# Float64 weights to float32: two activations and three integer steps in place of a masked reassembly

## The chip, the cores and the metric

The kernel runs on one core of a Trainium2 chip. The metric is the time of one execution on the device in microseconds; the runs shown are given by their median.

## The reference

Causal attention over 4 batches, 12 heads, 448 positions and head width 64 feeds a gated product: with x the attention's output as 1792 rows of 768,

```python
scores = scale * np.matmul(q, k.transpose(0, 1, 3, 2))      # causal mask, softmax, times v
a = x @ w_a          # 768 x 1536
b = x @ w_b          # 768 x 1536
return (a * b @ w_out).astype(np.float32)                   # 1536 x 768
```

q, k and v come as float32. The three weight matrices come as float64, since the setup multiplies float32 numbers by a float64 scalar.

## The kernel before

**Layout.** The weights are cut into 36 units of 128 partitions by 768 columns: 24 for w_a and w_b (a pair for each of 12 blocks of the inner width) and 12 for w_out. A unit arrives as 64-bit words, which the kernel reads as pairs of 32-bit words: `t.t[:, :, 0]` are the low words, `t.t[:, :, 1]` the high ones, each 8 bytes from the next.

**Conversion.** `convert_unit` (line 358) makes one float32 unit out of one float64 unit. Line 371 masks the exponent out of the high words, line 373 the fraction, and sets the hidden one; line 376 rebiases the exponent on ACT; line 378 adds the low words to the fraction as a floating-point number; line 380 puts the sign in front of the exponent; line 383 multiplies fraction and exponent. The result goes into `w_32`, and by DMA into `w_keep` in memory, from which later uses load it again. The buffers are rings: three for the 64-bit words (`w_64`), two for `w_e`, two for `w_m`, three for `w_32`. In the rows of the trace below, buffer numbers and what follows them are left out, so `w_64` and `w_32` both read `w`.

**Splitting and products.** `split` (line 396) makes each float32 weight into a high part (`w_hi`, copied on ACT, line 315) and the remainder (`w_lo`, subtracted on DVE, line 331). `products` (line 742, the matmul is line 746) then does three passes for each block of 128: high times high, high times low, low times high. The activations are split in the same manner.

**Stages.** Up to about 90 us the attention of batches 0 and 1 runs (`scores`, `turn`, `values`): scores on PE, maxima on DVE (line 492), exponentials on ACT (line 498), scaling on ACT or POOL (lines 520 and 521), transposes on PE (line 554) with their copies on ACT or DVE (lines 315 and 323), and products with v (lines 576 and 598). From about 67 us the products of these batches with the weights begin, use by use (`uses`, line 1007), and the attention of batches 2 and 3 is woven in between them, one pair of heads for every twelve steps (`attend`, line 1070), until about 244 us. Behind that there are products alone. In each use of the first half one unit is converted for a use soon to come (`convert_next`) and, by the table `EXTRA`, in twelve of them one more, whose result is only stored for later.

**Order.** Nothing is issued in program order. Each operation is noted with its engine, a planned duration, what it reads and writes, and (for DVE operations that share a port with POOL) the mode "x". `Plan.order` (line 142) is a list scheduler: it runs through the planned durations and picks for each engine, in general, the earliest operation in program order among those that are ready. The order that it finds is then issued as it is, so on the chip each engine executes a fixed sequence. Loads and stores go through SP's queue, sums into memory through POOL's.

Of the kernel before, what the change touches and what calls it, by code (L numbers as in the profile page):

```python
# [9 lines left out]
F32 = mybir.dt.float32  # L10
F32R = mybir.dt.float32r
U32 = mybir.dt.uint32
AF = mybir.ActivationFunctionType
ALU = mybir.AluOpType
# [4 lines left out]
P = 128  # L19
# [6 lines left out]
UW = KT * P  # L26
# [229 lines left out]
def causal_attention_then_gated_product(  # L256
# [9 lines left out]
    nc = tc.nc  # L266
    plan = Plan()
# [4 lines left out]
    def sb(tag, n, shape, dt=F32):  # L272
        return plan.ring(tag, n, lambda i: sbuf.tile(shape, dt, tag=f"{tag}{i}", name=f"{tag}{i}"))
# [32 lines left out]
    w_m = sbuf.tile([P, 2, UW], U32, tag="w_m", name="w_m")  # L306
# [27 lines left out]
    def load(nbytes, o, i, reads, writes, by=None):  # L334
        plan.op("sp", dma_ns(nbytes), lambda: (by or nc.sync).dma_start(out=o(), in_=i()), reads, writes)
# [6 lines left out]
    w_64, w_32, w_parts = [], [], []  # L342
# [14 lines left out]

    def convert_unit(besides=False):
        u, t = w_64.pop(0)
        e, m, wt = sb("w_e", 2, [P, UW], U32), plan.ring("w_m", 2, lambda i: w_m[:, i]), sb("w_32", 3, [P, UW])  # L360

        def low():
            return t.t[:, :, 0]

        def high():
            return t.t[:, :, 1]

        def r():
            return m.t.bitcast(F32)

        plan.op("dve", 470, lambda: nc.vector.tensor_scalar(  # L371
            out=e.t, in0=high(), scalar1=0x7FF00000, scalar2=None, op0=ALU.bitwise_and), [t], [e], "x")
        plan.op("dve", 470, lambda: nc.vector.tensor_scalar(
            out=m.t, in0=high(), scalar1=0x000FFFFF, scalar2=0x00100000,
            op0=ALU.bitwise_and, op1=ALU.bitwise_or), [t], [m], "x")
        plan.op("act", 735, lambda: nc.scalar.activation(  # L376
            e.t, e.t, AF.Copy, bias=-896.0 * 2**23, scale=8.0), [e], [e])
        plan.op("dve", 869, lambda: nc.vector.scalar_tensor_tensor(
            out=r(), in0=m.t, scalar=2.0**32, in1=low(), op0=ALU.mult, op1=ALU.add), [m, t], [m], "x")
        plan.op("dve", 869, lambda: nc.vector.scalar_tensor_tensor(  # L380
            out=e.t, in0=high(), scalar=0x80000000, in1=e.t,
            op0=ALU.bitwise_and, op1=ALU.bitwise_or), [t, e], [e], "x")
        plan.op("dve", 869, lambda: nc.vector.scalar_tensor_tensor(  # L383
            out=wt.t, in0=r(), scalar=2.0**-52, in1=e.t.bitcast(F32),
            op0=ALU.mult, op1=ALU.mult), [m, e], [wt], "x")
        load(P * UW * 4, lambda: w_keep[u], lambda: wt.t, [wt], [("keep", u)])
        if not besides:
            w_32.append(wt)
# [371 lines left out]
    def convert_one(besides=False):  # L760
        convert_unit(besides)
        load_next()
# [430 lines left out]
```

## Time and profile before

| what | value |
|---|---|
| median of the 3 runs shown | 617.97 us |
| lowest and highest | 617.84 and 619.04 us |
| span of the profiled execution | 616.9 us |
| median less that span | 1.1 us |
| PE busy | 610.7 us (99%) |
| DVE busy | 550.2 us (89%) |
| ACT busy | 385.7 us (63%) |
| POOL busy | 81.9 us (13%) |
| conversions: first and last start on DVE | 31.7 and 364.3 us |

The span runs from the first to the last instruction of one profiled execution, whose own time is not listed apart from it; the 1.1 us are how far the median of the runs stands above it. Busy times are sums over the whole span, and the stages differ: a share of the whole says little about any one of them. The ends of matmuls are modelled, so a busy PE is not by itself PE at its peak.

### The profile page before, as it was taken

Reading aid. Unit: us, or ns where it says so; the run is one execution under the profiler, and the core shown is the slowest. Engines: PE = TensorE matmul, PEld = TensorE weight load, DVE = VectorE, ACT = ScalarE, POOL = GpSimd, SP = SyncE. Lnnn points to the kernel's source line nnn. Section 1 sums busy time; section 2 is a strip of 40 time slices with the busy share of each in tenths; the row PEclk is TensorE's granted clock in tenths of the full one; section 3 lists DMA queues with packets and bytes.
Section 4 is the critical chain, followed back from the end, with each engine's and each line's share of the span. In section 5 each row is a group of like instructions: output and inputs, shape, how many; then the busy total and the mean of one; then the engine's idle time right before and its main releaser. Section 6 shows DMA issues by size and latency. Waiting matters only on the chain.

```text
span 616.9 us, 11539 instructions
## 1 busy us (share of the span) xinstructions
PE 610.7 (99%) x4027; PEld 543.1 (88%) x4027; DVE 550.2 (89%) x1237; ACT 385.7 (63%) x932; POOL 81.9 (13%) x140
## 2 busy tenths in 40 slices
PE   8999999999999999999999999999999999999997
PEld 6666778888888888999999999999999999999997
DVE  7799999999999999899889996788999768889984
ACT  6989969978898887454445545344455434455530
POOL 3775112210011111000000122000000000000030
PEclk9999999999999999999999999999999999999999
DMA  8879889687776778972122678321113432122354
GB/s 312 255 180 290 233 246 316 187 284 241 250 261 210 257 262 311 340 260 78 53 76 100 173 167 172 81 68 62 52 52 120 154 112 76 52 74 78 104 91 100
DMA packets 46858, 104.70 MB, mean 170 GB/s; under 512 B 5456, under 2 KB 31440, under 8 KB 46800
## 3 DMA queue, kind: packets, MB, share of 16 engines
q1 hardware_dynamic: 41904, 96.16, 47.2%
q0 software_dynamic: 4608, 7.34, 8.5%
q8 instruction: 32, 0.52, 0.3%
q10 hardware_dynamic: 288, 0.46, 0.2%
q14 instruction: 26, 0.21, 0.1%
HBM read 70.52 MB, written 33.42 MB: 168 GB/s over the span
## 4 chain that ended last, share of the span: by engine, by line
PE 96%; ACT 2%; DVE 1%; DMA 1%; issue 0%
PE m L746 66%; PE t L746 7%; PE t L554 6%; PE s L746 4%; PE pv L576 3%; PE s L483 3%; PE t L483 2%; PE pv L746 2%; PE m L598 2%; PE pv L598 1%; ACT p L498 1%; PE m L483 1%; ACT early L498 1%; DMA raw<-kT 1%; DVE w_e L371 0%; ACT pt L315 0%
## 5 line engine op out<-in xcount | busy, mean ns | idle before, releaser
L746 PE MATMUL m<-x_hi,w_hi 128*128 128x448 f32 x360 | 134.8, 374 | 0.0
L746 PE MATMUL m<-x_hi,w_lo 128*128 128x448 f32 x360 | 130.6, 363 | 0.0
L746 PE MATMUL m<-x_lo,w_hi 128*128 128x448 f32 x360 | 130.1, 361 | 0.0
L315 ACT ACTIVATE w_hi<-w 128x384 fp32r<-128x384 f32 (+1 forms) x96 | 57.5, 599 | 31.0 <-PE m L746 13.1
L746 PEld LDWEIGHTS m<-x_hi,w_lo 128*128 128x128 f32 x360 | 67.5, 188 | 5.0
L746 PEld LDWEIGHTS m<-x_hi,w_hi 128*128 128x128 f32 x360 | 67.6, 188 | 4.5 <-issue 0.2
L746 PEld LDWEIGHTS m<-x_lo,w_hi 128*128 128x128 f32 x360 | 67.6, 188 | 4.0
L315 ACT ACTIVATE mid<-m 128x448 f32<-128x448 f32 x72 | 38.9, 540 | 51.0 <-PE m L746 43.4
L498 ACT ACTIVATE p<-p,st 128x448 f32<-128x448 f32 (+6 forms) x126 | 62.5, 498 | 9.7 <-DVE st L492 9.6
L315 ACT ACTIVATE w_hi<-w_e_s 128x384 fp32r<-128x384 f32 x72 | 37.3, 521 | 45.8 <-PE m L746 25.0
L331 DVE TENSOR_TENSOR w_lo<-w,w_hi 128x384 fp32r<-128x384 f32 (+1 forms) x96 | 63.0, 656 | 2.6 <-ACT w_hi L315 2.6
L340 POOL DMA_DIRECT2D out<-mid x20 | 17.6, 898 | 347.5 <-ACT mid L315 335.2
L521 POOL TENSOR_SCALAR p<-p,st 128x256 f32<-128x256 f32 (+6 forms) x56 | 38.6, 726 | 136.8 <-ACT p L498 69.5
L746 PE MATMUL m<-g_hi,w_hi 128*128 128x448 f32 (+2 forms) x150 | 54.6, 364 | 0.0
L746 PE MATMUL m<-g_hi,w_lo 128*128 128x448 f32 (+2 forms) x150 | 53.8, 359 | 0.0
L746 PE MATMUL m<-g_lo,w_hi 128*128 128x448 f32 (+2 forms) x150 | 53.7, 358 | 0.0
L331 DVE TENSOR_TENSOR w_lo<-w_e_s,w_hi 128x384 fp32r<-128x384 f32 x72 | 39.9, 554 | 13.9 <-ACT w_hi L315 13.3
L315 ACT ACTIVATE pt<-t 128x512 f32<-128x512 f32 x72 | 39.8, 575 | 9.2 <-PE t L554 8.7
L746 PE MATMUL m<-p_x,w_hi 128*128 128x448 f32 x144 | 43.7, 363 | 0.0
L315 ACT ACTIVATE g_hi<-mid 128x448 fp32r<-128x448 f32 x42 | 24.1, 575 | 21.9 <-DVE mid L331 21.9
L380 DVE SCALAR_TENSOR_TENSOR w_e<-w,w_e 128x768 uint32<-128x768 uint32 x36 | 34.7, 965 | 0.7 <-ACT w_e L376 0.5
L383 DVE SCALAR_TENSOR_TENSOR w<-w_m,w_e 128x768 f32<-128x768 f32 x36 | 35.3, 979 | 0.0
(182 smaller groups left out, 1478.2 us busy)
## 6 DMA issues: line engine op xcount, KB each, us to landing
w<-w SPq DMA_DIRECT2D x36, 768.0 KB, 6.2
w<-w_keep SPq DMA_DIRECT2D x48, 384.0 KB, 3.1
w_keep<-w SPq DMA_DIRECT2D x36, 384.0 KB, 5.2
raw<-qT SPq DMA_DIRECT2D x24, 224.0 KB, 4.1
raw<-kT SPq DMA_DIRECT2D x22, 224.0 KB, 4.5
v<-v SPq DMA_DIRECT2D x24, 192.0 KB, 4.3
out<-mid SPq DMA_DIRECT2D x20, 224.0 KB, 3.9
out<-mid POOLq DMA_DIRECT2D x20, 224.0 KB, 4.2
```

The costliest lines, as they stand in the source:

```text
L315: return nc.scalar.activation(o(), i(), AF.Copy)
L331: plan.op(engine, ns, lambda: e.tensor_tensor(out=o(), in0=a(), in1=b(), op=op), reads, writes, "f" if banks.intersection(reads) else "x")
L340: lambda: nc.gpsimd.dma_start(out=o(), in_=i(), accum_op=ALU.add), reads, writes, "d")
L380: plan.op("dve", 869, lambda: nc.vector.scalar_tensor_tensor(out=e.t, in0=high(), scalar=0x80000000, in1=e.t, op0=ALU.bitwise_and, op1=ALU ...
L383: plan.op("dve", 869, lambda: nc.vector.scalar_tensor_tensor(out=wt.t, in0=r(), scalar=2.0**-52, in1=e.t.bitcast(F32), op0=ALU.mult, op1=A ...
L483: x = nc.tensor.matmul(at[r][0].t[to * D:(to + 1) * D, at[r][1]], q[:, r * D:(r + 1) * D], k[:, 0:D * (r + 1)], start=True, stop=True)
L498: return nc.scalar.activation(view(r), view(r), AF.Exp, bias=st.t[:, nm, r:r + 1], scale=-1.0, accum_out=st.t[:, sm, r:r + 1],)
L521: return nc.gpsimd.tensor_scalar(out=view(r), in0=view(r), scalar1=st.t[:, rc, r:r + 1], scalar2=1.0, op0=ALU.mult, op1=ALU.mult)
L554: x = nc.tensor.matmul(t.t[:, P * i:P * (i + 1)], of, swapped if rs[0] in CROSSED else ident, is_transpose=True, start=True, stop=True,)
L576: r = nc.tensor.matmul(ps.t[j * D:(j + 1) * D, 128 * c:S], vt.t[:, c, j, :], parts[n].t[:, j, o:o + count, :].rearrange("p i d -> p (i d)" ...
L598: r = nc.tensor.matmul((ps, more)[row].t[j * D:(j + 1) * D, at:at + count * D], v, parts[n].t[rows, j, o:o + count, :].rearrange("p i d -> ...
L746: r = nc.tensor.matmul(ps.t[:, at], a[:, i, :], x()[:, at], start=first and n == 0, stop=last and n == 2, skip_group_check=part)
```

## The change

The unit is converted in another way. ACT reads the high words as float32 numbers and scales them by 2 to the power of -112, which moves the exponent's bias, and reads the low words as integers and scales them by 2 to the power of -29, rounded to integers. DVE shifts the scaled high words left by 3 bits, puts the sign bit of the high words in front, and adds the rounded low words as integers. There are two ACT operations where there was one, and three DVE operations where there were five. The buffers and their rings stay, with `w_e` holding the rounded low words; the planned durations are those of like operations before. The store into `w_keep` and all that uses the units stay as they are.

```diff
     def convert_unit(besides=False):
         u, t = w_64.pop(0)
-        e, m, wt = sb("w_e", 2, [P, UW], U32), plan.ring("w_m", 2, lambda i: w_m[:, i]), sb("w_32", 3, [P, UW])
-
-        def low():
-            return t.t[:, :, 0]
+        y, m, wt = sb("w_e", 2, [P, UW], U32), plan.ring("w_m", 2, lambda i: w_m[:, i]), sb("w_32", 3, [P, UW])
 
         def high():
             return t.t[:, :, 1]
 
-        def r():
-            return m.t.bitcast(F32)
-
+        plan.op("act", 735, lambda: nc.scalar.activation(
+            m.t.bitcast(F32), high().bitcast(F32), AF.Copy, scale=2.0**-112), [t], [m])
+        plan.op("act", 735, lambda: nc.scalar.activation(y.t, t.t[:, :, 0], AF.Copy, scale=2.0**-29), [t], [y])
         plan.op("dve", 470, lambda: nc.vector.tensor_scalar(
-            out=e.t, in0=high(), scalar1=0x7FF00000, scalar2=None, op0=ALU.bitwise_and), [t], [e], "x")
-        plan.op("dve", 470, lambda: nc.vector.tensor_scalar(
-            out=m.t, in0=high(), scalar1=0x000FFFFF, scalar2=0x00100000,
+            out=m.t, in0=m.t, scalar1=3, scalar2=None, op0=ALU.logical_shift_left), [], [m], "x")
+        plan.op("dve", 869, lambda: nc.vector.scalar_tensor_tensor(
+            out=m.t, in0=high(), scalar=0x80000000, in1=m.t,
             op0=ALU.bitwise_and, op1=ALU.bitwise_or), [t], [m], "x")
-        plan.op("act", 735, lambda: nc.scalar.activation(
-            e.t, e.t, AF.Copy, bias=-896.0 * 2**23, scale=8.0), [e], [e])
-        plan.op("dve", 869, lambda: nc.vector.scalar_tensor_tensor(
-            out=r(), in0=m.t, scalar=2.0**32, in1=low(), op0=ALU.mult, op1=ALU.add), [m, t], [m], "x")
-        plan.op("dve", 869, lambda: nc.vector.scalar_tensor_tensor(
-            out=e.t, in0=high(), scalar=0x80000000, in1=e.t,
-            op0=ALU.bitwise_and, op1=ALU.bitwise_or), [t, e], [e], "x")
-        plan.op("dve", 869, lambda: nc.vector.scalar_tensor_tensor(
-            out=wt.t, in0=r(), scalar=2.0**-52, in1=e.t.bitcast(F32),
-            op0=ALU.mult, op1=ALU.mult), [m, e], [wt], "x")
+        plan.op("dve", 869, lambda: nc.vector.tensor_tensor(
+            out=wt.t.bitcast(U32), in0=m.t, in1=y.t, op=ALU.add), [m, y], [wt], "x")
         load(P * UW * 4, lambda: w_keep[u], lambda: wt.t, [wt], [("keep", u)])
```

## Rows read from the trace of the kernel before

**Rows 1.** The page: span, and busy us, share and instructions of PE's line.
```profile
span 616.9 us, 11539 instructions
...
PE 610.7 (99%) x4027; PEld 543.1 (88%) x4027; DVE 550.2 (89%) x1237; ACT 385.7 (63%) x932; POOL 81.9 (13%) x140
```

**Rows 2.** The chain that ended last, in order of time: start, us, what.
```profile
244.55 28.01 PE m L746 x139
...
272.59 186.19 PE m L746 x929
```

**Rows 3.** Stages: length; busy us of PE, PEld, DVE, ACT, POOL; clock, DMA, GB/s.
```profile
36.00:67.40 31.40, 31.40 (x333) 21.22 (x330) 30.62 (x108) 28.90 (x92) 17.74 (x32) 1.00 0.87 234
67.40:92.20 24.80, 24.80 (x179) 19.90 (x178) 23.35 (x42) 20.24 (x50) 2.57 (x3) 1.00 0.91 253
92.20:244.50 152.30, 152.30 (x1332) 133.89 (x1329) 146.48 (x353) 133.62 (x346) 23.24 (x25) 1.00 0.77 257
244.50:280.00 35.50, 35.48 (x180) 32.91 (x177) 32.43 (x57) 18.05 (x35) 0.00 (x0) 1.00 0.81 282
```

**Rows 4.** Waits of PE's weight loads, 20 to 245 us: total us, times, longest.
```profile
PEld s L483 <- issue: 7.0, 41, 0.2
...
PEld t L554 <- ACT pt L315: 1.2, 1, 1.2
...
PEld t L554 <- DVE st L492: 0.2, 1, 0.2
...
PEld s L483 <- DMA raw<-kT: 0.2, 1, 0.2
```

**Rows 5.** DVE in order of time, around 31 and 228 us: start, us, instruction.
```profile
31.69 1.97 DVE L371 TENSOR_SCALAR w_e<-w 128x768 uint32<-128x768 uint32 x1
...
227.34 0.95 DVE L383 SCALAR_TENSOR_TENSOR w<-w_m,w_e 128x768 f32<-128x768 f32 x1
228.21 0.56 DVE L371 TENSOR_SCALAR w_e<-w 128x768 uint32<-128x768 uint32 x1
228.68 0.56 DVE L373 TENSOR_SCALAR w_m<-w 128x768 uint32<-128x768 uint32 x1
```

**Rows 6.** ACT in order of time, around 114 us.
```profile
114.16 1.57 ACT L376 ACTIVATE w_e<-w_e 128x768 uint32<-128x768 uint32 x2
```

**Rows 7.** Groups by line and shape: count, busy us, mean ns; idle before.
```profile
L315 ACT ACTIVATE w_hi<-w 128x384 fp32r<-128x384 f32 x72 | 37.3, 518 | 27.5 <-PE m L746 11.7 <-PE t L746 10.6 <-ACT w_hi L315 2.7
...
L383 DVE SCALAR_TENSOR_TENSOR w<-w_m,w_e 128x768 f32<-128x768 f32 x36 | 35.3, 979 | 0.0
L378 DVE SCALAR_TENSOR_TENSOR w_m<-w_m,w 128x768 f32<-128x768 uint32 x36 | 35.1, 974 | 0.1
...
L376 ACT ACTIVATE w_e<-w_e 128x768 uint32<-128x768 uint32 x36 | 30.1, 841 | 4.4 <-DVE w_e L371 4.2
...
L331 DVE TENSOR_TENSOR w_lo<-w,w_hi 128x768 fp32r<-128x768 f32 x24 | 23.2, 965 | 0.0
...
L373 DVE TENSOR_SCALAR w_m<-w 128x768 uint32<-128x768 uint32 x36 | 20.3, 564 | 0.0
L315 ACT ACTIVATE w_hi<-w 128x768 fp32r<-128x768 f32 x24 | 20.2, 840 | 3.5 <-DVE w L383 1.7 <-PE m L746 1.4 <-PE t L483 0.3
```

**Rows 8.** Stages, line 376 on ACT alone: busy us (instructions); clock, DMA, GB/s.
```profile
36.00:67.40 31.40, 1.68 (x2) 1.00 0.87 234
67.40:92.20 24.80, 4.20 (x5) 1.00 0.91 253
92.20:244.50 152.30, 19.14 (x23) 1.00 0.77 257
```

**Rows 9.** Waits of SP's queue, 92.2 to 244.5 us.
```profile
SPq L335 <- DVE w_e L380: 32.3, 12, 6.4
```

**Rows 10.** Waits of ACT, 92.2 to 244.5 us.
```profile
ACT p L498 <- DVE st L492: 6.4, 11, 1.5
ACT pt L315 <- PE t L554: 6.4, 11, 1.6
```

## The prediction

> **What bounds the kernel now.** I read the page first. PE is busy 610.7 of 616.9 us [rows 1], but the ends of matmuls are modelled, so that figure doesn't show that PE is at its limit. The chain of waits in order of time does. From 244.55 us on it is PE alone: 929 matmuls in 186.19 us are 0.2004 us each, behind 139 in 28.01 us at 0.2015 [rows 2]. The reader is to see that nothing but matmuls is left to shorten there: whatever the change does after 244 us costs and gains nothing unless PE is made to wait.
>
> Next the table by stage [rows 3]. From 36 to 244.5 us PE's busy time equals the length of each stretch, and the waits of PE's weight loads [rows 4] say the same from 20 us on: the longest sum, 7.0 us in 41 pieces, is "issue" (it waited for no other engine), the longest wait for ACT is one of 1.2 us, for DVE one of 0.2 us, for a DMA one of 0.2 us. So PE is the bound from about 20 us to the end, and the conversion's first instruction comes at 31.7 us [rows 5]. Before that the change has nothing to touch.
>
> The same table shows what stands close behind PE. In the long stretch from 92.2 to 244.5 us, where the second half of the attention is woven into the products, DVE is busy 146.48 of 152.30 us (96.2%) and ACT 133.62 us (87.7%). In the stretch after it ACT is busy 18.05 of 35.50 us.
>
> **The change, part by part.** Profiled durations overlap the next instruction's start, so I price an instruction by its distance to the next one. On DVE a scalar_tensor_tensor of 768 columns takes 228.21 - 227.34 = 0.87 us and a tensor_scalar 228.68 - 228.21 = 0.47 us [rows 5]. On ACT two conversions in a row take 1.57 us, of which the last shows its full 0.84: 0.73 us each [rows 6].
>
> *DVE, removed*: two tensor_scalar and three scalar_tensor_tensor per unit, 2 x 0.47 + 3 x 0.87 = 3.55 us. *DVE, added*: one shift (tensor_scalar), one scalar_tensor_tensor, one tensor_tensor add. No shift and no integer add is in the trace. The shift is nearest to the masks, also 32-bit tensor_scalar of 768 columns, one of them 564 ns [rows 7]: 0.47 us; if it ran at the pace of the two-input instructions, 0.87. The add is nearest to the tensor_tensor of 768 columns at 965 ns [rows 7]: 0.87 us. New sum 0.47 + 0.87 + 0.87 = 2.21 us (bound above 2.61). DVE loses 1.34 us per unit (0.94 at least). In the long stretch 23 units pass [rows 8]: 23 x 1.34 = 30.8 us, and DVE falls from 146.48 to about 116 us of 152.3.
>
> *ACT, removed*: one activation per unit, 0.73 us. *ACT, added*: two, the scaling of the high words and the rounding of the low ones. Both are Copy with a scale over 768 columns, like the one removed (841 ns) and like the split of a weight at 840 ns [rows 7], but they read every second word, 8 bytes apart, which no ACT row here does from SBUF. On DVE a read of that step costs nothing: the instruction that reads the low words takes 974 ns, the one with three contiguous operands 979 [rows 7]. I take 0.73 us each, so ACT gains 0.73 us per unit. The bound above is ACT at half pace: 384 more columns cost 840 - 518 = 322 ns [rows 7], so 768 column times more are 0.64 us an instruction.
>
> ACT's sum by stretch, with the units of [rows 8] and the busy times of [rows 3]: 36 to 67.4 us, 28.90 + 2 x 0.73 = 30.4 of 31.4 us; 67.4 to 92.2, 20.24 + 5 x 0.73 = 23.9 of 24.8; 92.2 to 244.5, 133.62 + 23 x 0.73 = 150.4 of 152.3, that is 98.8%. So the change moves the place of the nearest engine behind PE from DVE to ACT, and nearer than DVE was. Of ACT and DVE together the long stretch loses 14 us of work.
>
> What hides the added ACT work is PE's own stream. PE needs ACT for the exponentials, the transposes' copies and the weight splits, but products of weights already split lie between them, and a conversion is needed only uses later. Without that cover the cost would be all of what ACT can't hold.
>
> The Trainium skill speaks on both sides here. "ScalarE: Activation LUTs", section "Rules for kernel authors", gives a plain multiply to VectorE rather than ScalarE, and the rows agree in direction: 0.47 us on DVE against 0.73 on ACT. "Perfetto Trace Analysis", section "Optimizing Scalar/DVE Operations", allows the move when DVE is saturated. By the first rule the change puts work on the dearer engine, by the second on the freer one; the sum above goes by the rows, where DVE at 96.2% is still not what PE waits for.
>
> **Waits and queues.** The order of each engine is made anew from the planned costs, so the whole interleaving between 30 and 280 us can shift. Each conversion used to begin on DVE and visit ACT in its middle; now it begins on ACT, which needs only the loaded words, and ends with three DVE steps in a row. An activation that waits (for the load, or for a buffer of w_m or w_e that two units before still hold) has exponentials and PSUM copies queued behind it on ACT, and PE waits for those. On SP the next load of 64-bit words waits for the last reader of the old ones: 32.3 us in 12 waits for line 380 [rows 9], with the attention's loads queued behind. After the change that reader is the sign step on DVE (or the rounding on ACT, if it is later), which two DVE steps fewer precede. I cost this at nothing, covered as now by loads issued early: PE waits 0.2 us for DMAs in all [rows 4]; if the cover were gone, it would be the longest of these waits, 6.4 us, once. The stores of the converted weights don't move.
>
> What could be gained: ACT now idles 6.4 us for the maxima from DVE and 6.4 us for transposes from PE in the long stretch [rows 10]. A relieved DVE takes away the former, and this is what makes room for the new activations.
>
> **The rivals.** *Hidden (my forecast).* PE stays fed. For: ACT's work still fits into every stretch, the freed DVE shortens ACT's own waits, and DVE at 96.2% costs PE next to nothing today. I add one uncovered activation, 0.73 us, in the stretch from 36 us on, where few products are ready yet (between 0 and the two units' 1.46): 616.9 + 0.7 = 617.6 us of span, or with the 1.1 us by which the median 617.97 stands above the profiled span, 618.7.
>
> *ACT becomes the bound (other side: slower).* Place: 92.2 to 244.5 us. If ACT can be kept busy there no better than DVE is now, its 150.4 us take 150.4 / 0.962 = 156.3 us: 4.0 us more, 622.0. The same comes out if only the 6.4 us that it waits for transposes stay: 156.8, or 4.5 more. It decides as soon as ACT idles more than 152.3 - 150.4 = 1.9 us there. For: today it idles 18.7 us in that stretch, and each engine executes a fixed order, in which PE must stop at a late transposition even with products behind it. Against: conversions need nothing but loaded words, so they fill ACT's gaps; late ACT work can move past 244.5 us, where 17 us are idle. Upper bound, if both waits of [rows 10] stay: 163.2, or 10.9 more.
>
> *The strided reads slow ACT.* 2 x 0.644 us per unit make 23 x 1.288 = 29.6 us more, ACT needs 180.0 us in the stretch, 27.7 too many: about 646. Against: the DVE rows above. The Trainium skill has a rule by which this happens: "Vector Engine (DVE) Microarchitecture Reference", section "5.2 Measured stream behaviour on trn2 (trn3 not measured)", wants runs of two adjacent words for the full rate. The rows of the strided DVE reads don't bear it out at this step, and for ACT no row here shows it.
>
> *Faster.* A lighter DVE would have to end waits of PE. All of PE's waits for other engines between 20 and 245 us are a few us at most, those for DVE 0.2 us apiece [rows 4]; a luckier order might give back 1.5 us: 616.5.
>
> **How the numbers follow.** Hidden 0.50, ACT bound 0.38, strided reads 0.04, faster 0.08. About 0.2%, 1.2 us, is what a measurement here can tell from no change (the three runs shown lie between 617.84 and 619.04). Hidden lies within it (617.2 to 619.2 by its own bounds); the ACT bound and the strided reads are slower, 0.42 together; faster 0.08. The predicted time is that of the hidden case, 618.7. The range goes from 617.2, which leaves out most of the faster cases, to 623.0, which takes in the ACT bound at 622.0 and 622.5 and leaves out its far end and the strided case.
>
> **What would show it.** Right: two new activations at about 0.84 us each, the shift at about 0.56, sign and add at about 0.96; DVE near 116 us of the long stretch, ACT near 150; PE's waits for ACT still about 1 us a piece and few. Wrong: in the long stretch, waits of PE's transposes or value products for ACT (p, pt) that sum to several us and a later start of the matmul run that now begins at 244.55 us would show ACT as the bound; activations of 1.4 us or more the strided reads; a start of that run well before 243 us would show a gain that I don't see.

## The result, and the profile after

The changed kernel takes 626.15 us where the kernel before takes 618.31 on the same chip: a ratio of 1.0122, interval 1.0108 to 1.0136. The forecast was 618.7 with a range up to 623.0, so the time is outside the range, on the slower side. One execution of 2165 us is left out of this ratio, and because the first profile fell on it, the one shown here is of the same kernel measured again: 626.5 us, 1.0123 (1.0108 to 1.0138).

First the page of the changed kernel: span and busy times, to be read against [rows 1].

```profile
span 624.7 us, 11540 instructions
...
PE 614.7 (98%) x4027; PEld 543.4 (87%) x4027; DVE 505.4 (81%) x1165; ACT 413.5 (66%) x968; POOL 75.3 (12%) x140
```

The span is 7.8 us longer, DVE 44.8 us lighter, ACT 27.8 us heavier. Over the whole span both engines look far from full. The groups of the new conversion (count, busy us, mean ns, idle before) answer to [rows 7]:

```profile
L370 DVE SCALAR_TENSOR_TENSOR w_m<-w,w_m 128x768 uint32<-128x768 uint32 x36 | 36.0, 1004 | 0.8
L373 DVE CUSTOM_DVE_ANT_0 w<-w_m,w_e 128x1536 uint16<-128x1536 uint16 x36 | 34.8, 968 | 11.5 <-ACT w_e L367 11.3
L365 ACT ACTIVATE w_m<-w 128x768 f32<-128x768 f32 x36 | 33.1, 920 | 0.3 <-DVE w L373 0.3
L367 ACT ACTIVATE w_e<-w 128x768 uint32<-128x768 uint32 x36 | 32.9, 915 | 0.0
L368 DVE TENSOR_SCALAR w_m<-w_m 128x768 uint32<-128x768 uint32 x36 | 20.6, 575 | 14.5 <-ACT w_m L365 14.2
```

Shift, sign and add cost about what was forecast. The activations take 920 and 915 ns where 841 were forecast. ACT in order of time shows their pitch (the distance from one start to the next), 244.56 - 243.76 = 0.80 us, against 0.73 from [rows 6]:

```profile
243.76 0.92 ACT L365 ACTIVATE w_m<-w 128x768 f32<-128x768 f32 x1
244.56 0.91 ACT L367 ACTIVATE w_e<-w 128x768 uint32<-128x768 uint32 x1
```

The stages (columns as in [rows 3], which they answer to, with two stretches more):

```profile
36.00:67.40 31.40, 31.18 (x320) 20.21 (x320) 28.85 (x103) 31.28 (x93) 16.55 (x31) 1.00 0.96 272
67.40:92.20 24.80, 24.80 (x170) 19.94 (x170) 17.54 (x34) 21.91 (x55) 3.76 (x4) 1.00 0.78 200
92.20:244.50 152.30, 152.03 (x1315) 132.76 (x1308) 118.61 (x305) 150.03 (x366) 16.85 (x25) 1.00 0.79 253
244.50:280.00 35.50, 33.50 (x190) 29.41 (x189) 23.98 (x42) 20.06 (x38) 0.00 (x0) 1.00 0.75 285
...
170.00:210.00 40.00, 40.00 (x352) 34.50 (x347) 31.46 (x86) 39.83 (x103) 3.57 (x6) 1.00 0.81 257
...
264.00:290.00 26.00, 22.56 (x107) 19.49 (x107) 18.80 (x37) 11.39 (x24) 0.00 (x0) 1.00 0.38 135
```

In the long stretch ACT is busy 150.03 us (forecast 150.4) and DVE 118.61 (forecast about 116); in 170 to 210 us ACT is busy 39.83 of 40.00 us. ACT is also full in 36 to 67.4 us: 31.28 of 31.40 us, where 30.4 was forecast. Yet PE's line stays nearly full in all of these. PE's idle time stands in the last row, 26.00 - 22.56 = 3.4 us, in a stretch where ACT is busy less than half the time. The same stretch of the kernel before:

```profile
264.00:290.00 26.00, 25.98 (x130) 23.93 (x129) 24.59 (x49) 14.10 (x29) 0.00 (x0) 1.00 0.47 161
```

All matmuls have one shape there, so their number tells more than PE's modelled line: 107 against 130, and 23 x 0.2004 [rows 2] = 4.6 us of work that isn't done.

The number also shows losses where PE's line is full. Matmuls of the products alone up to 210 us (length; PE's busy us and matmuls; clock, DMA, GB/s), in the kernel before and the changed one, and in two versions that are explained below, with the new conversion for the first seven units alone and for all but these:

```profile
0.00:210.00 210.00, 96.74 (x426) 1.00 0.81 253
0.00:210.00 210.00, 94.12 (x416) 1.00 0.82 250
0.00:210.00 210.00, 93.65 (x412) 1.00 0.82 253
0.00:210.00 210.00, 96.26 (x425) 1.00 0.82 253
```

All four have run the same 1457 other matmuls by then, so 10 x 0.2004 = 2.0 us are lost in the changed kernel, 2.8 us with the first seven alone, and 0.2 us with all but these. Now the chain that ended last, in order of time, against [rows 2]:

```profile
250.59 21.06 PE m L735 x105
272.76 0.62 DVE v_x L331
...
280.09 1.00 ACT w_hi L315 x2
281.59 0.63 DVE acc L331
282.35 71.89 PE m L735 x358
...
507.96 72.00 PE m L735 x360
```

Before, matmuls alone followed from 244.55 us on. Now they begin 6.04 us later, at 250.59, and they run out at about 271.7. Until 282.35 the chain goes through DVE and ACT, and PE has only short groups of matmuls; this is called the hole below. The last 360 matmuls are the same work in both kernels; before, they began here:

```profile
500.18 72.00 PE m L746 x360
```

So 507.96 - 500.18 = 7.8 us have been lost by then, which is the whole difference of the spans, and nothing is lost behind it. In the front, the attention of batches 0 and 1 up to about 92 us, the chain differs too. In the kernel before it runs through PE alone from 35.0 to 92 us. In the changed kernel it leaves PE from 39.79 to 58.92 us: it goes through DVE's maxima, and from 50.12 us on mostly through ACT's exponentials and copies, with steps of the conversion in between, of which these are two:

```profile
42.83 0.96 DVE w_m L370
...
53.22 0.82 ACT w_m L365
```

What PE waits for between 264 and 290 us (total, times, longest):

```profile
PE m L735 <- DVE acc L331: 1.6, 1, 1.6
PE m L735 <- DVE w_lo L331: 0.9, 2, 0.5
PE m L735 <- ACT mid L315: 0.7, 1, 0.7
PE m L735 <- ACT w_hi L315: 0.3, 1, 0.3
```

These are the splits and sums that prepare the next products, not conversions. Their work starts with reloads of earlier results into buffers that the attention frees as it ends. SP's issues of these in the kernel before, and then in the changed one:

```profile
244.71 1.75 SPq L335 DMA_DIRECT2D pt<-x_first  x4
...
263.31 0.91 SPq L335 DMA_DIRECT2D pt<-x_first  x2
```

```profile
250.70 1.89 SPq L335 DMA_DIRECT2D pt<-x_first  x4
...
267.61 3.93 SPq L335 DMA_DIRECT2D out<-mid  x3
271.64 0.87 SPq L335 DMA_DIRECT2D pt<-x_first  x2
```

The group of four goes out 6.0 us later, just as the attention ends 6 us later, and the last pair 8.3 us later, at the moment when PE runs out of ready products. Two more things show on the way to this last pair. DVE waited 3.50 us for an earlier pair of reloads to land:

```profile
267.43 0.62 DVE L331 TENSOR_TENSOR pt<-pt,pt 128x448 f32<-128x448 f32 x1 [3.50 <-DMA pt<-x_first]
```

And in SP's fixed order the last pair stands behind three stores of outputs, the third of which was sent at 271.20 us, when ACT had copied a finished product. In the kernel before two of these stores come behind the last pair. What of the delay is owed to the order of SP's queue was not tried by itself.

While ACT was late, PE ran ahead with products that were ready: by 244.5 us it had run 534 matmuls of the products, against 535 before, but 41 fewer of all others. That debt falls due here.

So of the 7.8 us 4.6 are lost between 264 and 290 us. The other 3.2 us had been lost before, in stretches in which PE's modelled line shows next to nothing: 2.0 of them by 210 us.

### The profile page after: what moved, and what is told of

Same layout as the page of the kernel before. It is cut to its first block, busy times and chain, and to the rows that moved or that the text cites. A ratio compares the mean times of both kernels' runs of the same rounds, so it can differ in the third digit from the quotient of the medians.

```text
span 2163.5 us, 11540 instructions
## 1 busy us (share of the span) xinstructions
PE 2157.8 (100%) x4027; PEld 1237.9 (57%) x4027; DVE 518.3 (24%) x1165; ACT 425.6 (20%) x968; POOL 74.6 (3%) x140
## 3 DMA queue, kind: packets, MB, share of 16 engines
q1 hardware_dynamic: 41904, 96.16, 13.5%
## 4 chain that ended last, share of the span: by engine, by line
PE 99%; issue 0%; ACT 0%; DVE 0%
PE m L735 66%; PE t L543 7%; PE t L735 7%; PE pv L565 4%; PE s L735 4%; PE s L472 3%; PE pv L735 2%; PE t L472 2%; PE pv L587 2%; PE m L472 2%; PE m L587 2%; PE fill L1115 0%; DVE acc L331 0%; ACT mid L315 0%; ACT p_x L315 0%
## 5 line engine op out<-in xcount | busy, mean ns | idle before, releaser
L735 PE MATMUL m<-x_hi,w_hi 128*128 128x448 f32 x360 | 367.3, 1020 | 0.7 <-ACT mid L315 0.7
L735 PE MATMUL m<-x_hi,w_lo 128*128 128x448 f32 x360 | 356.5, 990 | 0.0
L735 PE MATMUL m<-x_lo,w_hi 128*128 128x448 f32 x360 | 355.8, 988 | 0.0
L735 PEld LDWEIGHTS m<-x_lo,w_hi 128*128 128x128 f32 x360 | 160.3, 445 | 92.5 <-issue 92.1
L735 PE MATMUL m<-g_hi,w_hi 128*128 128x448 f32 (+2 forms) x150 | 149.7, 998 | 0.0
L735 PE MATMUL m<-g_hi,w_lo 128*128 128x448 f32 (+2 forms) x150 | 146.3, 975 | 0.0
L735 PE MATMUL m<-g_lo,w_hi 128*128 128x448 f32 (+2 forms) x150 | 146.2, 975 | 0.0
L735 PE MATMUL m<-w_x,w_hi 128*128 128x448 f32 x108 | 97.3, 993 | 0.0
L543 PE MATMUL t<-ident,p 128*128 128x128 f32 x144 | 91.1, 707 | 0.0
L735 PE MATMUL m<-p_x,w_lo 128*128 128x448 f32 x90 | 88.3, 982 | 0.0
```

Of the source, the lines that this page charges most:

```text
L543: x = nc.tensor.matmul(t.t[:, P * i:P * (i + 1)], of, swapped if rs[0] in CROSSED else ident, is_transpose=True, start=True, stop=True,)
L735: r = nc.tensor.matmul(ps.t[:, at], a[:, i, :], x()[:, at], start=first and n == 0, stop=last and n == 2, skip_group_check=part)
```

## The experiments

Every ratio is to the kernel before on the same chip. ACT and DVE are busy times in the long stretch, "idle" is 45.50 us less PE's busy time in 244.5 to 290 us (by the modelled line, which shows less than the matmuls' number does), and "last 360" is the start of the last 360 matmuls. The runs shared a chip in fours, in the order of the table, and the last three by themselves.

| kernel | us | ratio (95%) | ACT | DVE | idle | last 360 |
|---|---|---|---|---|---|---|
| before | 618.3 to 619.1 | 1 | 133.62 | 146.48 | 0.0 | 500.18 |
| the change | 626.5 | 1.0123 (1.0108 to 1.0138) | 150.03 | 118.61 | 3.6 | 507.96 |
| low words rounded on DVE | 622.83 | 1.0063 (1.0048 to 1.0078) | 133.90 | 134.60 | 0.1 | 504.02 |
| before, one activation more | 626.34 | 1.0109 (1.0084 to 1.0135) | 146.86 | 144.57 | 2.8 | 509.89 |
| change, copies shared | 621.44 | 1.0038 (1.0023 to 1.0053) | 144.51 | 135.25 | 0.0 | 502.87 |
| before, replanned | 619.61 | 1.0022 (1.0013 to 1.0031) | 134.34 | 145.31 | 0.4 | 501.09 |
| change, replanned | 626.09 | 1.0121 (1.0098 to 1.0144) | 148.98 | 116.66 | 1.9 | 507.16 |
| new for the first 7 units | 624.37 | 1.0090 (1.0072 to 1.0108) | 134.36 | 145.05 | 2.1 | 505.55 |
| old for the first 7 | 627.40 | 1.0142 (1.0126 to 1.0159) | 149.52 | 120.46 | 4.4 | 507.91 |
| copies shared, replanned | 619.79 | 1.0028 (1.0015 to 1.0040) | 145.72 | 135.13 | 0.0 | 501.24 |
| old first, shared, replanned | 618.49 | 0.9999 (0.9990 to 1.0008) | 144.92 | 134.84 | 0.0 | 499.88 |
| extra units earlier | 622.21 | 1.0057 (1.0042 to 1.0072) | 150.62 | 120.62 | 0.6 | 504.07 |
| words in a row | 625.92 | 1.0116 (1.0101 to 1.0131) | 148.27 | 118.61 | 3.4 | 506.25 |
| old first, shared | 619.81 | 1.0018 (1.0005 to 1.0031) | 145.08 | 136.11 | 0.0 | 501.59 |
| before, copies shared | 631.96 | 1.0214 (1.0194 to 1.0234) | 118.33 | 147.47 | 6.8 | 514.23 |
| old first, half new | 619.02 | 1.0008 (0.9998 to 1.0018) | 145.71 | 140.44 | 0.0 | 500.50 |

The theory: ACT is full, so the attention and all that waits for its buffers come late. The rivals: the slower reads of every second word; a worse order found by the scheduler; the new instructions on DVE.

### Is it ACT's load?

The first four ran together. The changed kernel again, without any edit:

> The changed kernel itself, for a profile at the same pace of PE as the profile of before. Measured against before: about 7.8 us slower. If ACT has become the bound: ACT busy over 97% somewhere between 36 and 250 us, PE waiting there for ACT (exponentials, scaling, copies of transposes, splits) by some 7 us in sum, and the run of pure matmuls beginning some 7 us later than 244.55 us; each new activation about 0.84 us. If the strided reads are slow: the new activations, or the one on the high words, at 1.2 us or more. If only the new interleaving costs: PE without waits for ACT but with more and shorter runs of its kinds of matmul, and ACT with idle time left.

It repeated the result and gave the rows above. The waits for ACT of some 7 us didn't come: between 20 and 245 us those of PE's matmuls sum to 1.4 us, and those of its weight loads [rows 4] to 3.8, against 3.1 before. Then the change with the rounding of the low words on DVE, so that ACT has one activation per unit, as before:

```diff
-        plan.op("act", 735, lambda: nc.scalar.activation(y.t, t.t[:, :, 0], AF.Copy, scale=2.0**-29), [t], [y])
+        plan.op("dve", 470, lambda: nc.vector.tensor_scalar(
+            out=y.t, in0=t.t[:, :, 0], scalar1=2.0**-29, scalar2=None, op0=ALU.mult), [t], [y], "x")
```

> The rounding of the low words goes from ACT to DVE as a tensor_scalar; the rest of the change stays. ACT then has one conversion activation per unit, as before the change, and DVE 2.7 us per unit instead of 3.55. If ACT's load is the cause: back within 1.5 us of 618. If it is the order of steps (ACT first, three DVE steps in a row) or the integer steps: it stays at 622 or more. If the strided read of the high words is slow: it keeps at least half of the 7.8 us.

622.83 us: half of the loss comes back and the hole at 264 to 290 us closes. The step takes 598 ns on DVE instead of 915 on ACT. The Trainium skill's "ScalarE: Activation LUTs", section "Rules for kernel authors", gives such a plain multiply to VectorE, and this run agrees, by time as well. But 3.8 us stay although ACT is as light as before. By what was expected that speaks for the order or the integer steps, not for ACT's load alone. They are lost in the front: a group of twelve transposes that starts at 90.55 us in the kernel before starts 3.9 us later here.

```profile
94.50 0.90 PE t L473 x12
```

Third, the old conversion with one more activation per unit, whose result is overwritten at once:

```diff
+        plan.op("act", 735, lambda: nc.scalar.activation(r(), high().bitcast(F32), AF.Copy, scale=2.0**-112), [t], [m])
```

> The kernel before with one activation more per unit, the scaling of the high words into w_m, whose result is overwritten by the mask that follows; all of the old conversion stays, on DVE too. If one more activation per unit is by itself what costs: slower by about 8 us (626), or more, since DVE keeps its 3.55 us. If it is not the load of ACT: within 1.5 us of 618.

626.34 us (four executions from 624.6 to 628.4, the profile of the slowest): one more activation alone costs as much as the whole change, with the old work on DVE all still there. The place differs. PE idles 31.40 - 30.10 = 1.3 us in 36 to 67.4 us, where ACT is no fuller than before (28.89 us); ACT is full in 67.4 to 92.2 us (24.36 of 24.80); and PE idles where the attention ends, 19.50 - 16.69 = 2.8 us. The activation also puts a wait for ACT between two DVE steps of the conversion, and this run doesn't tell that wait from the load.

```profile
36.00:67.40 31.40, 30.10 (x308) 19.84 (x306) 28.74 (x96) 28.89 (x89) 18.17 (x32) 1.00 0.89 243
67.40:92.20 24.80, 24.32 (x167) 18.96 (x164) 20.67 (x49) 24.36 (x62) 2.59 (x3) 1.00 0.77 202
244.50:264.00 19.50, 16.69 (x101) 14.12 (x100) 16.20 (x25) 11.96 (x20) 0.00 (x0) 0.91 0.96 337
```

Fourth, the change with ACT relieved elsewhere: ACT's copies of the transposes of batches 2 and 3 out of PSUM are shared with DVE, as in batches 0 and 1.

```diff
-TAKE = (("act", "dve"), ("act", "dve"), ("act", "act"), ("act", "act"))
+TAKE = (("act", "dve"), ("act", "dve"), ("act", "dve"), ("act", "dve"))
```

> The changed kernel with one of the two copies of transposes per turn of batches 2 and 3 moved from ACT to DVE (0.48 us each, two per pair of heads, 12 pairs: 11.5 us of ACT's work between 92 and 244 us, against the 16.8 us that the change added). If ACT is the bound in that stretch: most of the loss comes back, 618 to 620. If the loss arises before 92 us, or from the new order: 624 to 627.

621.44 us with all new activations in place, less of the loss back than was expected, but the hole is gone. The attention ends no earlier than in the changed kernel (its matmul run begins at 252.68 us), but the last pair of reloads goes out at 263.79 instead of 271.64:

```profile
264.00:290.00 26.00, 26.00 (x132) 24.18 (x131) 23.88 (x47) 13.49 (x28) 0.00 (x0) 1.00 0.38 119
```

```profile
263.79 0.82 SPq L335 DMA_DIRECT2D pt<-x_first  x2
```

So it is not the attention's end by itself that opens the hole. By these two runs it opens when the last reloads, which ACT and DVE work must free and follow, come later than PE's stock of ready products lasts.

### Is it the order, and which units?

The scheduler believes that an activation costs 735 ns. In the next four runs it was told 820 (first in the kernel before, whose activation it doesn't describe, then in the changed one), and the conversions were exchanged by count.

```diff
-        plan.op("act", 735, lambda: nc.scalar.activation(
+        plan.op("act", 820, lambda: nc.scalar.activation(
```

> The kernel before with one planned duration changed, that of its conversion activation, from 735 to 820 ns. The work is the same to the last instruction; only the order that the list scheduler finds can differ. If the loss of the changed kernel is work on ACT: within 1.5 us of the kernel before. If a new order by itself costs some us, since the constants were fitted to one order: 2 us or more slower.

> The changed kernel with both activations planned at 820 ns, the distance at which they really follow each other, in place of 735. If the orders are late because the plan took the activations for shorter than they are: 2 us or more come back (624 or less, on a day when the changed kernel takes 626.3). If ACT has simply too much work: 625 to 628.

The kernel before becomes 0.2% slower through another order of the same work, so an order alone is worth 1.4 us here. The changed kernel gains nothing that can be told from the truer plan, as was expected if ACT has too much work.

```diff
+        count, converted[0] = converted[0], converted[0] + 1
+        (convert_new if count < 7 else convert_old)(besides, u, t)
```

> The new conversion for the first 7 units only, those that are converted up to about 92 us, and the old one for the other 29. If the loss arises where ACT is full in the attention of batches 0 and 1: 2 to 3 us slower than before. If it arises in the long stretch: within 1 us of before.

> The other way round: the old conversion for the first 7 units, the new one for the other 29. If the long stretch and the debt that is paid at 270 to 285 us are the larger share: 4 to 6 us slower than before, with PE idle at 270 to 285 us again. If the loss is mostly in front: within 2 us of before.

The second of these has `count >= 7`. The first seven units alone, those up to 92 us [rows 8], cost 5.6 us; the other 29 alone 8.8; all of them 7.5. Both parts cost more than was expected, and they don't add. A little over 1 us of the second is TensorE's clock (0.93 in the second row; see the end). The 29 leave the front as it was and open the widest hole:

```profile
36.00:67.40 31.40, 31.40 (x333) 21.42 (x330) 30.63 (x107) 29.14 (x93) 17.51 (x31) 1.00 0.90 237
...
264.00:290.00 26.00, 21.58 (x98) 19.06 (x97) 18.94 (x37) 11.91 (x24) 0.00 (x0) 0.93 0.29 102
```

Here 98 matmuls run in place of 130, 6.4 us, and 0.2 us are lost by 210 us. The seven, on the other hand, cost although ACT in the long stretch is as before (134.36 us). PE loses 31.40 - 30.32 = 1.1 us in 36 to 67.4 us, 2.8 us by 210 us in the number of matmuls, and it idles 2.1 us in the hole: a loss in the front is enough to make the late reloads later (the last pair goes out at 268.56 us, against 263.31 before).

### Do the remedies add up?

The change with both edits, copies shared and activations planned at 820; then the same with the old conversion for the first seven units. These are edits already shown.

> The changed kernel with both corrections: one of the two copies of transposes per turn of batches 2 and 3 on DVE, and the activations planned at 820 ns. If front and long stretch are separate losses, each with its own cure: what the copies alone left in front (about 1.5 us up to 92 us) goes too, 618.5 to 620.5. If the losses are those of whatever order comes out: no better than the copies alone, 621 to 624.

> The old conversion for the first 7 units, the new one for the other 29 with the activations planned at 820 ns, and one copy of transposes per turn on DVE in batches 2 and 3. If ACT's load in the long stretch is what made the kernel with the old first 7 units slow (627): 617 to 620, with no idle time of PE at 264 to 290 us. If it is the order of steps: 622 or more.

619.79 and 618.49 us. The second equals the kernel before (618.53 beside it). PE has no hole in either, and behind the attention there is nothing left to gain: from 247.46 us on the second has 1053 matmuls at 211.02 us, 0.2004 us each, as in [rows 2]. Its 29 units have the new instructions on DVE, so these by themselves cost nothing.

Next, three of the extra conversions moved from the tenth to twelfth use into the first three:

```diff
-EXTRA = (0, 0, 0, 1, 1, 1, 1, 1, 1, 1, 1, 1, 1, 1, 1)
+EXTRA = (1, 1, 1, 1, 1, 1, 1, 1, 1, 0, 0, 0, 1, 1, 1)
```

> The changed kernel with three of the extra conversions moved from the uses 9 to 11 to the uses 0 to 2, so that ACT has less to do while the last pairs of the attention pass. If the idle time of PE at 270 to 282 us is a debt of the attention's late end: the attention ends at 248 us or before, PE idles less than 1.5 us between 264 and 290 us in place of 3.6, and the time is 622 to 625, front losses included. If that idle time has another cause: it stays at 3 us or more, 626 to 628.

622.21 us, more than half of the loss back, with ACT just as full in the stretch (150.62 us). The attention doesn't end by 248 us, as was expected, but at 250.17 (250.59 in the changed kernel); still the hole shrinks to 0.6 us. So ACT's total in the stretch doesn't decide alone; what else it has to do near the end of the attention may count too. This run also moves the order, and how much of its 4 us is that it can't tell.

### Is it the reads of every second word?

Both activations read 768 words in a row as integers instead of every second one, the first with a scale of 0; the weights are thus not converted.

```diff
-            m.t.bitcast(F32), high().bitcast(F32), AF.Copy, scale=2.0**-112), [t], [m])
-        plan.op("act", 735, lambda: nc.scalar.activation(y.t, t.t[:, :, 0], AF.Copy, scale=2.0**-29), [t], [y])
+            m.t.bitcast(F32), flat(0), AF.Copy, scale=0.0), [t], [m])
+        plan.op("act", 735, lambda: nc.scalar.activation(y.t, flat(1), AF.Copy, scale=2.0**-29), [t], [y])
```

> The changed kernel with both activations reading 768 words in a row instead of every second word; what they write is not the weight, so the output is not the reference's. If the 8-byte step is what makes them 911 to 918 ns instead of 841: 835 to 850 ns here, ACT's work falls by 23 x 0.16 = 3.7 us in the long stretch, and 1 to 5 us come back. If it is something else (two activations of one unit in a row, the 32-bit types): 900 ns or more.

```profile
L368 ACT ACTIVATE w_m<-w 128x768 f32<-128x768 uint32 x36 | 30.4, 844 | 0.2 <-DVE w L376 0.2
L370 ACT ACTIVATE w_e<-w 128x768 uint32<-128x768 uint32 x36 | 30.3, 842 | 0.0
```

The activations take what was forecast, 844 and 842 ns, so the 8-byte step costs some 75 ns of each. The time is 625.92 us: the 1 to 5 us that were expected back don't come, and the interval overlaps that of the change. Even with the forecast's own durations the loss is there.

### What is left: load or plan, ACT or any engine, dose

> Old conversion for the first 7 units, new one for the other 29, planned as in the change, and the copies of the transposes of batches 2 and 3 shared between ACT and DVE. If ACT's load is the cause, taking the copies away removes nearly all of the 8.8 us that the 29 units cost: 618.3 to 620, PE without idle time between 264 and 290 us, the reloads behind the attention at about 263 and 271 us. If the longer planned durations of the new activations were what brought the earlier version with both edits to the old time, this one stays above it by what they gave with the copies alone (621.4 less 619.8): 620 to 621.5, with the loss ahead of 245 us.

Old conversion for the first seven, copies shared, nothing replanned: 619.81 us against 627.40 without the copies. Moving the copies gives back 7.6 of the 8.8 us; the longer plans add 1.3 at most. So it is the load, and not the longer planned durations, that counts. (Moving the copies changes the order too; replanning alone moved 1.4 us at most.)

> The kernel before with nothing changed but that the copies of the transposes of batches 2 and 3 are shared between ACT and DVE. ACT falls from 133.6 to about 122 of 152.3 us in the long stretch, DVE's work there rises from 146.5 us by 12 to 16, over what the stretch holds. If an engine behind PE costs time as soon as its work overruns the stretch, whichever engine it is, the time is 623 to 628 and PE idles between 264 and 290 us. If it is ACT alone that hurts, because PE waits for ACT's exponentials and copies and DVE's share can be late, the time is 617.5 to 620.

The same edit in the kernel before, where DVE and not ACT is the fuller one, costs 13.5 us, more than was expected. The copies add 13.7 us to DVE's 146.48 of 152.30, 160.2 in all. DVE gets 147.47 us done there, ACT has 34 us of room, and PE waits for DVE's split:

```profile
92.20:244.50 152.30, 150.66 (x1284) 129.75 (x1278) 147.47 (x360) 118.33 (x315) 22.76 (x25) 1.00 0.71 235
...
260.00:265.00 5.00, 2.06 (x11) 1.59 (x9) 5.00 (x8) 2.46 (x4) 0.00 (x0) 1.00 0.93 291
265.00:270.00 5.00, 3.92 (x12) 3.56 (x13) 5.00 (x10) 1.94 (x4) 0.00 (x0) 0.68 1.00 351
```

```profile
266.08 0.48 PE L746 MATMUL m<-g_hi,w_lo 128*128 128x448 f32 x1 [4.02 <-DVE w_lo L331]
...
267.17 0.58 PE L746 MATMUL m<-g_hi,w_hi 128*128 128x448 f32 x1
267.54 0.58 PE L746 MATMUL m<-g_lo,w_hi 128*128 128x448 f32 x1
```

So nothing here is peculiar to ACT: each of the two engines behind PE, when given more than the stretch holds, opens such a hole. Last, every second unit after the seventh by the new conversion:

```diff
-        (convert_new if count >= 7 else convert_old)(besides, u, t)
+        (convert_new if count >= 7 and count % 2 else convert_old)(besides, u, t)
```

> Old conversion for the first 7 units; after that every second unit by the new one (14 or 15 of 29). ACT's work in the long stretch is about 143 to 145 of 152.3 us, halfway between 133.6 and 150 or more. If the loss comes only when ACT is full, it is gone: 618 to 620, no idle time of PE between 264 and 290 us. If each new conversion costs its share (8.8 us for 29), 622 to 624.

```profile
92.20:244.50 152.30, 152.22 (x1319) 133.44 (x1317) 140.44 (x339) 145.71 (x361) 25.48 (x25) 1.00 0.81 272
...
264.00:290.00 26.00, 26.00 (x132) 24.37 (x131) 23.99 (x48) 13.65 (x29) 0.00 (x0) 1.00 0.30 96
```

619.02 us, the time of the kernel before (1.0008, 0.9998 to 1.0018), where half of 8.8 would have made it 622.9. The loss doesn't grow with each conversion. It starts as ACT becomes full: with the front unchanged it is nothing at 145.71 us and 8.8 us at 149.52. Between the two nothing was tried.

## Why the prediction was wrong

**The durations held, but for one.** Shift 575 ns (forecast about 560), sign and add 1004 and 968 (about 960), DVE 118.61 us in the long stretch (about 116). The activations were taken at 0.73 us each and have a pitch of 0.80: the reads of every second word cost 75 ns, a ninth of what the strided rival priced (640). That rival was right in sign and worth next to nothing: without it the time is 625.92.

**The sum of ACT seems to hold, in part by luck.** 150.4 us were forecast in the long stretch and 150.03 measured. But with the real pitch ACT was asked for 133.62 + 23 x (2 x 0.80 - 0.73) = 153.6 us of 152.3. What didn't fit moved on: in 244.5 to 264 us ACT is busy 12.65 us, against 9.71 before. And in 36 to 67.4 us, where 30.4 us were forecast for two units, three units passed and ACT was full, 31.28 of 31.40 us.

**The step that failed is the cover**: "What hides the added ACT work is PE's own stream", and with it that PE would stay fed because ACT's work "still fits into every stretch". It fitted to 1.2%, and that was too tight. With the forecast's own pitch, which the run with words in a row had, the loss was the same. Products did lie between the attention's steps, and PE's line did stay full to 244 us. But they were taken from a stock, and what refills the stock (reloads into the buffers that the attention frees, then splits on DVE and ACT) came late once ACT was late. The forecast looked for the cost where ACT is full. More than half of it, 4.6 of 7.8 us, is paid at 264 to 290 us, where ACT has room, and where the forecast saw 17 idle us as a place to put late work. In its sum this stood at nothing.

**A second term was mis-sized**: the one uncovered activation in the front, 0.73 us. By the number of matmuls the changed kernel has lost 2.0 us by 210 us, nearly all of it the front's, since the version with the old conversion for the first seven units has lost 0.2. The chain there runs through DVE's maxima and ACT's exponentials, with conversion steps among them, where it ran through PE alone.

**What the forecast took for a sign that PE stays fed** was PE's busy time, equal to the length of each stretch [rows 3]. The changed kernel's line is just as full in 92.2 to 244.5 us (152.03 of 152.30) while its work falls behind, so that line can't show a loss of this kind.

**The rival "ACT becomes the bound"** named the engine, the place of the cause and the sign. Its price was 4.0 to 4.5 us, and 7.8 were lost. Its sum has no term for two things. One is the front: the first seven units, 7 x (2 x 0.80 - 0.73) = 6.1 us more on ACT, some of it where ACT was already at 28.90 of 31.40 us, cost 5.6 us by themselves. The other is the hole. Its sign to look for, waits of PE's transposes or value products for ACT that sum to several us, didn't come either: the matmuls' waits for ACT sum to 1.4 us, and PE ran products in the meantime. The other sign did, the matmul run that begins at 250.59 instead of 244.55.

**When DVE is full enough.** "Perfetto Trace Analysis" of the Trainium skill, section "Optimizing Scalar/DVE Operations", lets work move to ACT when DVE is saturated. The runs say what that has to mean here. At 146.48 of 152.30 us DVE cost PE nothing; every second conversion moved left both under 146 us, for no gain; all of them moved overfilled ACT, for a loss of 1.2%; the copies moved the other way overfilled DVE, for 2.1%.

**What couldn't be gained.** The gain that DVE's relief could bring was rightly put at nearly nothing: of all versions none is faster than the kernel before. The best, with 29 units converted the new way and no hole, has its time (0.9999).

**What stays open.** Why the front loses time: ACT's load, or the new order of the steps. The run with the rounding on DVE lost its 3.8 us there with ACT no fuller than before (29.09 of 31.40 us in 36 to 67.4 us), so load alone doesn't explain it, and the same work in another order is worth 1.4 us. The chain names DVE's maxima and ACT's exponentials, but no run changed the front's order alone. Open as well is how much of the hole is owed to ACT's own work and how much to the order of SP's queue and the landing of the reloads.

## What to carry to other kernels

Price a move of work between engines by the stage, and look at the receiver: here a second engine could fill about 146 of 152.3 us without PE noticing (ACT 145.71 in one run, DVE 146.48 in the kernel before), and a plan that fits at 98.8% doesn't fit. A wait that isn't seen in the stage where an engine is full may be paid after it, so follow what the stage releases (buffers, reloads, splits) to where the bounding engine's stock runs out. Where a busy line is modelled, count the work done by a given time, in both kernels. Where a scheduler makes the order, run a change with the same work and another plan beside it: what such a reshuffle moves is the least that a change must move to mean something.

## What was not expected of the hardware

The integer addition of 768 words shows in the trace as a custom operation on 1536 halves of 16 bits, at 968 ns: no dearer than the float tensor_tensor of 768 columns at 965 [rows 7].

TensorE's clock fell after the longer waits for products. In the kernel before with copies shared PE stood idle for 4.02 us up to 266.08; from 266.8 to 270.2 us its matmuls then come every 0.37 us instead of 0.20, with a granted clock of 0.68 in 265 to 270 us, so they ran at the lower of the two levels, 1.2 GHz. Nine matmuls at 0.17 us more are some 1.5 us, on top of the hole. The same shows with the old conversion for the first seven units: behind waits of 2.36 and 1.38 us the granted clock is 0.93 in 264 to 290 us, and seven matmuls from 278.5 to 281.1 us come every 0.37 us. It shows behind a wait of 2.4 us in the kernel before with one activation more (0.91 in 244.5 to 264 us), and behind one of 1.9 us in the replanned change (0.93 in 264 to 290 us). In the changed kernel the idle time came in pieces of 1.6 us at most, and the granted clock stayed at 1.00.
